# A fused attention and gated-MLP kernel: which VectorE steps GpSimd's pieces wait for, with the order of all engines made anew

## The chip, the core and the metric

The kernel runs on one core of a Trainium2 chip. Five engines of that core work side by side and meet by semaphores: TensorE (PE, with its weight loads shown as PEld), VectorE (DVE), ScalarE (ACT), GpSimd (POOL) and SyncE (SP), which here issues nearly all DMAs. The metric is the device time of one execution in microseconds.

## The reference, cut to what matters

Eight batches of eight heads, 576 positions, head size 64; inputs are float32. Attention has a decay that comes from the running sum of log f, and its output goes through a gated MLP whose gate is a causal convolution of five taps.

```python
def _attn_ref(q, k, v, f):
    ...
    scores = scale * np.matmul(q, k.transpose(0, 1, 3, 2))
    log_f = np.log(np.clip(f, 0.0001, 1.0))
    cum = np.cumsum(log_f, axis=-1)
    decay = cum[:, :, :, None] - cum[:, :, None, :]
    scores = np.where(causal, -1000000000.0, scores + decay)
    ...
    attn = attn / (np.sum(attn, axis=-1, keepdims=True) + 1e-09)
    return np.matmul(attn, v).astype(np.float32)

def _moe_ref(x, w_val, conv_w, w_out):
    ...
    for k in range(K):
        gate_pre += conv_w[k][None, None, :] * xp[:, k:k + S, :]
    gate = 1.0 / (1.0 + np.exp(-gate_pre))
    val = x @ w_val
    return (gate * val @ w_out).astype(np.float32)
```

## The kernel before, in words

The 64 heads are worked as 32 pairs; one pair fills the 128 partitions. The program is a list of some 2350 steps, each a small Python function that issues one or a few instructions. Each pair i goes through these steps, named by their class in the code:

- S: PE multiplies q and k into PSUM banks in 64-row blocks and adds the decay, which it takes as a product of the selector pk with st, three bf16 pieces of the scaled running sum. For the first pair these two are apart (S and Sd).
- red: VectorE's custom instruction (L423) applies the mask and takes the row maximum (negm). SX: ScalarE takes the exponential (L427) into P and sums it into zs.
- DT: VectorE turns P in 32x32 blocks into T (L462). UC: two copies of T's halves into U (L248, on ACT, POOL or DVE), and U: four DMAs of the other halves.
- rec: 1e-9 is added to the sums (L435, on POOL or DVE); VectorE takes the reciprocal (L439) and turns it into zt (L440). zD and zB: DMAs that spread the reciprocals over zb.
- PV: PE multiplies U and v. X: VectorE multiplies the result by zb into x (L519).
- xh and xl: x is split into a part that PE takes in one pass and the rest (L248, L528). conv, cvm, cva: the five taps of the gate, one product (L255 on POOL and DVE, L253 on ACT) and one addition (L564 on POOL) each, or both in one on VectorE (L562). tanh: ScalarE.

After every fourth pair a batch is complete: Mv multiplies xh and xl with w_val, H (L595) applies the gate, hh and hl split the result (L609), Mo multiplies with w_out, O empties the bank and OD stores it. At the start come the steps on f: the clip and the running sum (class st0, L325 and L337), their scaling on ACT, and three casts with two subtractions in between (cast, L248, and st0, L345); for the last eleven pairs the same is done once more in the middle of the program (sts[1]), from a copy in DRAM (lnf). The two weight matrices are decoded from their int32 halves in many steps of ACT, VectorE and POOL (wv and wo; L695 to L711), beside the first pairs.

The order in which the steps are issued is neither a loop nor decided by the chip. A packed table, ORDER, holds for each place in the program the number of a step and the engine that does it (for those steps that may go to more than one), and behind that the PSUM banks. Every engine works through its own instructions strictly in that order and halts at the first whose semaphores are not there.

One rule is added when the steps are issued. PORT is a set of class names. The last VectorE instruction of such a class so far is kept in turn, and the first instruction of every POOL step gets a semaphore wait for it:

```python
        if e == "POOL" and turn is not None:
            tc.add_manual_dep(done[0], turn.name, wait, reason="shared port")
        elif e == "DVE" and cls in PORT:
            turn = done[-1]
```

Before, the class rec covers the addition of 1e-9 and also VectorE's step of reciprocal and turn, so a POOL step that comes behind such a step in the table waits for its turn zt (L440). The classes st0 and cast are not in the set.

Of the kernel before, what the change touches and what calls it, by code (L numbers as in the profile page):

```python
# [90 lines left out]
)
# [702 lines left out]
```

## Time and profile before

| | us |
| --- | --- |
| median of three timed runs | 459.16 (458.07 to 460.58) |
| profiled execution | 463.08 |
| its span, first to last instruction | 461.0 |
| mean granted TensorE clock | 0.981 |

The durations below come from the one profiled execution, which took 3.9 us more than the median. A row in order of time gives start and duration in us, the engine, the line, what was written from what, and in brackets how long the engine had stood idle before and on whom it had waited. A busy PE is not PE at its peak, since matmuls are pipelined and their ends are modelled.

### The profile page before, as it was taken

Reading aid. Unit: us, or ns where it says so; the run is one execution under the profiler, and the core shown is the slowest. Engines: PE = TensorE matmul, PEld = TensorE weight load, DVE = VectorE, ACT = ScalarE, POOL = GpSimd, SP = SyncE. Lnnn points to the kernel's source line nnn. Section 1 sums busy time; section 2 is a strip of 40 time slices with the busy share of each in tenths; the row PEclk is TensorE's granted clock in tenths of the full one; section 3 lists DMA queues with packets and bytes.
Section 4 is the critical chain, followed back from the end, with each engine's and each line's share of the span. In section 5 each row is a group of like instructions: output and inputs, shape, how many; then the busy total and the mean of one; then the engine's idle time right before and its main releaser. Section 6 shows DMA issues by size and latency. Waiting matters only on the chain.

```text
span 461.0 us, 16758 instructions
## 1 busy us (share of the span) xinstructions
PE 423.9 (92%) x6640; PEld 359.9 (78%) x6640; DVE 382.9 (83%) x1034; ACT 332.3 (72%) x836; POOL 309.4 (67%) x310
## 2 busy tenths in 40 slices
PE   6648998899999999999969898999999999999996
PEld 6427777787888788898858677988787988999985
DVE  5998987998997798999869888899777879976851
ACT  5786996999886878987667868677678878654131
POOL 7476756678884868787536889589579888572210
PEclk9797999999999999999989999999999999999999
DMA  8748879848695767987773587768587686845013
GB/s 287 283 129 249 213 190 241 198 118 261 186 248 163 209 171 197 274 232 206 211 199 100 136 239 215 219 181 204 132 246 192 188 206 173 223 118 129 23 70 114
DMA packets 74847, 87.23 MB, mean 189 GB/s; under 512 B 48145, under 2 KB 48145, under 8 KB 74769
## 3 DMA queue, kind: packets, MB, share of 16 engines
q1 hardware_dynamic: 74624, 85.87, 67.7%
q8 instruction: 52, 0.85, 0.9%
q10 hardware_dynamic: 144, 0.29, 0.2%
q14 instruction: 27, 0.21, 0.2%
HBM read 52.29 MB, written 10.26 MB: 136 GB/s over the span
## 4 chain that ended last, share of the span: by engine, by line
PE 47%; POOL 13%; DVE 13%; DMA 12%; issue 6%; SPq 5%; ACT 3%; POOLq 0%; DVEq 0%; ACTq 0%
PE banks L233 47%; POOL gate L564 6%; SPq L260 5%; DMA zb<-zd 4%; DVE banks L423 4%; DVE T L462 3%; DMA U<-T 2%; DMA vt<-in_v_dram 2%; POOL xl L528 2%; POOL U L248 2%; ACT P L427 2%; DMA sh<-in_w_val_dram 1%; POOL tm L255 1%; DMA zd<-zt 1%; DMA tm<-lnf 1%
## 5 line engine op out<-in xcount | busy, mean ns | idle before, releaser
L427 ACT ACTIVATE P<-banks,negm 128x384 f32<-128x384 f32 (+8 forms) x288 | 149.6, 528 | 46.4 <-DVE negm L423 36.4
L564 POOL TENSOR_TENSOR gate<-gate,tm 128x576 f32<-128x576 f32 x82 | 117.5, 1434 | 42.6 <-DVE tm L255 14.7
L423 DVE CUSTOM_DVE_ANT_0 banks<-banks,mk 128x512 f32<-128x512 f32 (+8 forms) x288 | 135.1, 504 | 9.6 <-PE banks L233 6.7
L462 DVE STREAM_TRANSPOSE T<-P 128x1088 f32<-128x1088 f32 (+2 forms) x96 | 110.9, 1166 | 6.6 <-DMA U<-T 3.5
L233 PE MATMUL banks<-xh,wall 128*128 128x288 f32 x512 | 108.8, 298 | 1.7 <-ACT P L427 0.9
L233 PE MATMUL banks<-Xr 64*64 64x288 f32 (+8 forms) x1280 | 103.2, 410 | 2.5 <-DMA Xr<-in_x_dram 2.5
L233 PEld LDWEIGHTS banks<-U,vt 64*64 64x64 f32 x3456 | 92.3, 136 | 14.1 <-issue 10.1
L233 PE MATMUL banks<-U,vt 64*64 64x128 f32 (+1 forms) x3456 | 93.2, 257 | 9.6 <-ACT sh L695 4.0
L233 PE MATMUL banks<-wall,hh 128*128 128x512 f32 x288 | 91.6, 399 | 0.0
L233 PEld LDWEIGHTS banks<-xh,wall 128*128 128x128 f32 x512 | 84.3, 189 | 6.0 <-ACT P L427 1.6
L233 PE MATMUL banks<-xl,wall 128*128 128x288 f32 x256 | 76.0, 297 | 4.1 <-POOL xl L528 3.9
L233 PEld LDWEIGHTS banks<-Xr 64*64 64x64 f32 x1280 | 65.0, 134 | 15.8 <-issue 5.1
L233 PEld LDWEIGHTS banks<-wall,hh 128*128 128x128 f32 x288 | 52.3, 189 | 13.2 <-DVE negm L423 1.3
L233 PE MATMUL banks<-st,pk 64*64 64x288 bf16 (+8 forms) x640 | 48.6, 297 | 11.3 <-ACT P L427 6.5
L233 PE MATMUL banks<-wall,hl 128*128 128x512 f32 x144 | 56.9, 395 | 2.3 <-POOL hl L609 2.3
L427 ACT ACTIVATION_READ_ACCUMULATOR P<-banks,negm 128x1 f32 x288 | 58.4, 203 | 0.0
L248 ACT COPY U<-T 128x1440 f32<-128x1440 f32 x37 | 51.3, 1396 | 5.9 <-PE banks L233 5.2
L233 PEld LDWEIGHTS banks<-xl,wall 128*128 128x128 f32 x256 | 48.4, 189 | 5.4 <-POOL xl L528 4.1
L233 PEld LDWEIGHTS <-pk 64*64 64x64 bf16 x640 | 26.5, 107 | 29.6 <-issue 24.9
L609 POOL TENSOR_TENSOR hl<-h,hh 128x576 fp32r<-128x576 f32 (+2 forms) x39 | 40.9, 1068 | 11.5 <-DVE gate L562 4.4
L528 POOL TENSOR_TENSOR xl<-x,xh 128x576 fp32r<-128x576 f32 x24 | 34.7, 1446 | 15.9 <-DVE zt L440 10.4
L519 DVE TENSOR_TENSOR x<-banks,zb 128x256 f32<-128x256 f32 (+1 forms) x96 | 30.8, 345 | 11.5 <-PE banks L233 5.5
(103 smaller groups left out, 495.8 us busy)
## 6 DMA issues: line engine op xcount, KB each, us to landing
U<-T SPq DMA_DIRECT2D x128, 180.0 KB
Xr<-in_x_dram SPq DMA_DIRECT2D x64, 288.0 KB
vt<-in_v_dram SPq DMA_DIRECT2D x32, 320.0 KB
out_dram<-ot SPq DMA_DIRECT2D x36, 256.0 KB
vt<-in_v_dram SPq DMA_DIRECT2D x32, 256.0 KB
zb<-zd SPq DMA_DIRECT2D x64, 80.0 KB
zb<-zd SPq DMA_DIRECT2D x64, 64.0 KB
sh<-in_w_val_dram SPq DMA_DIRECT2D x2, 512.0 KB
```

Source lines behind the costliest of these rows:

```text
L233: nc.tensor.matmul(out, lhsT=lhsT, rhs=rhs, start=start, stop=stop)
L248: (eng.copy if eng is nc.scalar else eng.tensor_copy)(out=out, in_=in_)
L255: eng.tensor_scalar(out=out, in0=in_, scalar1=col, scalar2=0.0, op0=ALU.mult, op1=ALU.add)
L260: lambda e: (nc.sync if e == "SP" else nc.scalar).dma_start(out=out, in_=in_), reads, writes, dma=span)
L423: nc.vector.tensor_tensor_reduce(out=sl, in0=sl, in1=mk[:, S - ext:], op0=ALU.add, op1=ALU.min, scale=-0.125, scalar=3.0e38, accum_out=neg ...
L427: nc.scalar.activation(out=dst, in_=bank(key)[:, a0:a0 + ext], func=AF.Exp, bias=negm[r][:, col], scale=-1.0, accum_out=zs[r][:, col])
L462: nc.vector.transpose(out=bass.AP(Tt.tensor, Tt.offset + 32 * FB[js[0]], [pitch, (32, nk), (CW, 2), (1, 32)]), in_=Pt[u])
L519: nc.vector.tensor_tensor(out=bass.AP(to.tensor, to.offset, [to.ap[0], *dims, (1, D)]), in0=bank(keys[y])[:, D * first:D * last].rearrange ...
L528: any_("xl", {"POOL": 1.4, "DVE": 0.67}, p, lambda eng: eng.tensor_tensor(out=xl[s], in0=xv, in1=xh[s][:, :].bitcast(F32), op=ALU.subtract ...
L564: eng.tensor_tensor(out=gt, in0=gt, in1=to, op=ALU.add)
L609: eng.tensor_tensor(out=hl[jj][:, y:y + x1 - x0], in0=h2[jj % 2][:, x0:x1], in1=hh[jj][:, y:y + x1 - x0].bitcast(F32), op=ALU.subtract)
```

## The change

Three things: the set PORT gets st0, cast and a name vdup that no step has; VectorE's step of reciprocal and turn gets the class recT, which is not in the set; and ORDER is another table. A POOL step so no longer waits for reciprocals and their turn, and waits for VectorE's clip, running sum, casts and subtractions on f where they come ahead of it in the table. The addition of 1e-9 keeps its class rec.

```diff
-PORT = {"wv", "wo", "rec", "xh", "xl", "diag", "conv", "cvm", "cva", "hh", "hl", "UC"}
+PORT = {"st0", "cast", "vdup", "wv", "wo", "rec", "xh", "xl", "diag", "conv", "cvm", "cva", "hh", "hl", "UC"}
 NS = (21, 11)
 ORDER = (
...
-    "c-lQuTTB$`wyvtKzTd0w)%WWAy}SB;@2<Y14~RYp@-QGL5##~UohW*e0o{o(JP5-{1bG;clL&GWKp%v0Cj-Mt6gi0^I}vmeL3bkPB*J(SK~8d{?U{%A>tAbq>s#wv>xV"
...
+    "c-mD`c}QIOmae<hzVB7H_FMa2b!*?NZtW%y)Z~w7JJ8xbh{gxT_CYimXe)UTZ3onLAQ}f+<3M73pmqkL?LccBh{ge99Ec_j(PSW+JV@+3h{iuADeVVyFPGmv=X~co-#N"
...
         def turn():
             nc.vector.reciprocal(out=zr[r][:, 0:NN], in_=zr[r][:, 0:NN])
             nc.vector.transpose(out=zt[r], in_=zr[r])
-        dve("rec", 0.36, p, turn, [("zr", r)], [("zr", r), ("zt", r)])
+        dve("recT", 0.36, p, turn, [("zr", r)], [("zr", r), ("zt", r)])
```

What the new table does is read from the instructions of the two programs, engine by engine. First POOL at the start of the program. ident is the unit matrix, one a column of ones that L337 reads, mk the mask, pk and sel the selectors of the decay. Before:

```order
L283 AFFINE_SELECT ident<-ident 128x128
L293 MEMSET one 128x1
L363 MEMSET zr_93 128x32
L362 MEMSET x_99 128x4
L314 MEMSET mk 128x576
L317 AFFINE_SELECT mk<-mk 64x64 x2
L294 MEMSET ebias 128x1
L298 MEMSET pk 128x64
L299 MEMSET sel 128x4
L305 AFFINE_SELECT pk<-pk 128x21 x3
```

Now, from the last rows of pk on; sh and wall are the weight decoding, U the copy of T:

```order
L305 AFFINE_SELECT pk<-pk 128x11 x3
L309 AFFINE_SELECT sel<-sel 64x1 x2
L293 MEMSET one 128x1
L314 MEMSET mk 128x576
L317 AFFINE_SELECT mk<-mk 64x64 x2
L707 TENSOR_TENSOR wall<-sh 128x512
L701 TENSOR_TENSOR sh<-sh 128x512
L363 MEMSET zr_93 128x32
L363 MEMSET zr_94 128x32
L536 TENSOR_TENSOR tm<-ident,cw 128x640
```

The constant one has moved from ahead of the mask to behind the whole of pk and sel, and so have the mask and the first zr and x; the first weight piece is L707 instead of L701.

Second, POOL in the middle, around the second round of the steps on f; the numbers tell the buffers apart (xl3 is the low part of the last pair of batch 3, U1 and zr1 belong to the pair after the next). Before:

```order
L564 TENSOR_TENSOR gate_113<-gate_113,tm_78 128x576 x3
L528 TENSOR_TENSOR xl1_108<-x321_100,xh1_102 128x576
L435 TENSOR_SCALAR zr1_94<-zs1_92 128x9
L528 TENSOR_TENSOR xl2_109<-x320_99,xh2_103 128x576
L248 COPY U1_85<-T1_83 128x1440
L528 TENSOR_TENSOR xl3_110<-x321_100,xh3_104 128x576
L255 TENSOR_SCALAR gate_113<-x321_100,cw_65 128x576
L564 TENSOR_TENSOR gate_113<-gate_113,tm_78 128x576 x2
L609 TENSOR_TENSOR hl_1439<-h320_114,hh_1262 128x64
```

Now:

```order
L435 TENSOR_SCALAR zr0_93<-zs0_91 128x9
L528 TENSOR_TENSOR xl1_108<-x321_100,xh1_102 128x576
L255 TENSOR_SCALAR tm_78<-x320_99,cw_65 128x576
L564 TENSOR_TENSOR gate_113<-gate_113,tm_78 128x576 x2
L435 TENSOR_SCALAR zr1_94<-zs1_92 128x9
L248 COPY U1_85<-T1_83 128x1440 x2
L255 TENSOR_SCALAR gate_113<-x321_100,cw_65 128x576
L564 TENSOR_TENSOR gate_113<-gate_113,tm_78 128x576
L255 TENSOR_SCALAR tm_78<-x321_100,cw_65 128x576
```

The pieces xl2 and xl3 are no longer among POOL's, and both copies into U1 have come to stand there together.

Third, VectorE at the same place. Before (the second instruction of each L423 is left out, as it repeats):

```order
L519 TENSOR_TENSOR x321_100<-banks_122,zb1_98 128x2x2x64 x2
L337 SCALAR_TENSOR_TENSOR tm_78<-one_123,tm_78 128x576
L339 TENSOR_SCALAR ref1_125<-tm_78 128x1
L423 ISA banks_122,negm0_89<-banks_122,mk_73 128x128
L423 ISA banks_122,negm0_89<-banks_122,mk_73 128x256
L423 ISA banks_122,negm0_89<-banks_122,mk_73 128x448
L248 CAST st1_71<-tm_78 128x576
L423 ISA banks_122,negm0_89<-banks_122,mk_73 128x320
L345 SCALAR_TENSOR_TENSOR tm_78<-st1_71,sel_72,tm_78 128x576
L423 ISA banks_122,negm0_89<-banks_122,mk_73 128x64
L439 RECIPROCAL zr1_94<-zr1_94 128x9
L440 STREAM_TRANSPOSE zt1_96<-zr1_94 128x32
```

Now:

```order
L519 TENSOR_TENSOR x321_100<-banks_122,zb1_98 128x2x2x64
L519 TENSOR_TENSOR x321_100<-banks_122,zb1_98 128x64
L519 TENSOR_TENSOR x321_100<-banks_122,zb1_98 128x2x2x64
L423 ISA banks_122,negm0_89<-banks_122,mk_73 128x448
L439 RECIPROCAL zr1_94<-zr1_94 128x9
L440 STREAM_TRANSPOSE zt1_96<-zr1_94 128x32
L423 ISA banks_122,negm0_89<-banks_122,mk_73 128x64
L528 TENSOR_TENSOR xl3_110<-x321_100,xh3_104 128x576
L337 SCALAR_TENSOR_TENSOR tm_78<-one_123,tm_78 128x576
L339 TENSOR_SCALAR ref1_125<-tm_78 128x1
```

The reciprocal and its turn now come ahead of the running sum L337 instead of behind it, and so does xl3, which was POOL's.

## Rows read from the trace of the kernel before

**Rows 1.** The page's busy us, share of the span and instructions of each engine.
```profile
PE 423.9 (92%) x6640; PEld 359.9 (78%) x6640; DVE 382.9 (83%) x1034; ACT 332.3 (72%) x836; POOL 309.4 (67%) x310
```

**Rows 2.** Ten-us windows: stretch, length, busy us: PE, PEld, DVE, ACT, POOL.
```profile
10.00:20.00 10.00, 5.70 (x70) 4.00 (x65) 9.67 (x26) 7.38 (x16) 4.32 (x3) 0.71 1.01 374
230.00:240.00 10.00, 6.11 (x30) 5.29 (x29) 5.82 (x17) 7.18 (x17) 2.68 (x2) 0.83 0.87 229
```

**Rows 3.** Order of time, first 16 us (start, duration, engine, line, what).
```profile
2.69 0.15 POOL L298 MEMSET pk<- 128x64 bf16 x1
...
5.87 1.35 DVE L337 TENSOR_TENSOR_SCAN x<-one,gate 128x576 f32<-128x576 f32 x1
...
8.29 0.32 POOL L309 TENSOR_SCALAR_AFFINE_SELECT sel<-sel 64x1 f32<-64x1 f32 x2
...
9.66 0.46 DVE L248 CAST st<-gate 128x576 bf16<-128x576 f32 x1 [0.23 <-ACT gate L341]
...
10.25 1.95 DVE L345 SCALAR_TENSOR_TENSOR gate<-st,sel,gate 128x576 f32<-128x576 bf16 x1
...
10.29 1.29 POOL L701 TENSOR_TENSOR sh<-sh 128x512 f32<-128x512 f32 x1 [1.69 <-ACT sh L699]
...
12.23 1.43 DVE L248 CAST st<-gate 128x576 bf16<-128x576 f32 x1
...
13.77 0.82 DVE L345 SCALAR_TENSOR_TENSOR gate<-st,sel,gate 128x576 f32<-128x576 bf16 x1
...
15.13 1.43 PE L233 MATMUL banks<-st,pk 64*64 64x288 bf16 x20 [3.13 <-DVE st L248]
```

**Rows 4.** Order of time up to PE's first matmuls on U.
```profile
22.62 2.10 DVE L462 STREAM_TRANSPOSE T<-P 128x768 f32<-128x768 f32 x2
...
26.82 1.38 POOL L248 COPY U<-T 128x1440 f32<-128x1440 f32 x1 [2.54 <-DVE zt L440]
...
30.86 1.18 SPq L260 DMA_DIRECT2D U<-T  x2
...
36.79 4.98 PE L233 MATMUL banks<-U,vt 64*64 64x128 f32 x105 [4.03 <-ACT sh L695]
```

**Rows 5.** Order of time at PE's halt in the middle.
```profile
227.13 0.67 ACT L248 CAST xh<-x 128x576 fp32r<-128x576 f32 x1
...
232.90 0.21 DVE L440 STREAM_TRANSPOSE zt<-zr 128x32 f32<-128x32 f32 x1
...
233.26 1.45 POOL L528 TENSOR_TENSOR xl<-x,xh 128x576 fp32r<-128x576 f32 x1 [5.60 <-DVE zt L440]
...
234.77 0.40 PE L233 MATMUL banks<-xl,wall 128*128 128x288 f32 x1 [3.89 <-POOL xl L528]
```

**Rows 6.** Two-us windows after the halt; behind POOL the granted clock.
```profile
236.00:238.00 2.00, 2.00 (x7) 1.51 (x6) 0.46 (x1) 1.06 (x4) 0.00 (x0) 0.52 0.96 288
238.00:240.00 2.00, 2.00 (x11) 1.90 (x10) 0.14 (x1) 1.41 (x5) 0.00 (x0) 0.63 0.82 209
```

**Rows 7.** Waits of POOL: who waited for whom, us in total, times, longest.
```profile
POOL xl L528 <- DVE zt L440: 10.4, 5, 5.6
```

**Rows 8.** Waits of PE, same columns.
```profile
PE banks L233 <- POOL hl L609: 2.3, 1, 2.3
```

**Rows 9.** Lines L439 and L440: smallest, median, largest ns.
```profile
L439 DVE RECIPROCAL zr<-zr x32: 170/207/217, 26.3 to 411.6; 128x9 f32<-128x9 f32 x32
L440 DVE STREAM_TRANSPOSE zt<-zr x32: 210/211/215, 26.5 to 411.9; 128x32 f32<-128x32 f32 x32
```

**Rows 10.** Order of time where a reciprocal falls inside a POOL addition.
```profile
109.71 1.43 POOL L564 TENSOR_TENSOR gate<-gate,tm 128x576 f32<-128x576 f32 x1
...
110.16 0.17 DVE L439 RECIPROCAL zr<-zr 128x9 f32<-128x9 f32 x1
```

**Rows 11.** Costliest groups: the gate additions on POOL and on DVE.
```profile
L564 POOL TENSOR_TENSOR gate<-gate,tm 128x576 f32<-128x576 f32 x82 | 117.5, 1434 | 42.6 <-DVE tm L255 14.7
L562 DVE SCALAR_TENSOR_TENSOR gate<-x,cw,gate 128x576 f32<-128x576 f32 x38 | 32.2, 855 | 6.1 <-POOL gate L564 5.8
```

More of the change, by code (lines that the diff above doesn't have):

```diff
@@ new lines @@
+    "5G|Bz2iQORghkh-Zm)U?X&kbecFx+9dCiC#V=00(oEswTCJNzb5XJtEd>Inb=88gZCM~P`kissurvO&wy!4h|*7OBR(hHBh^ytsrBG6b(Fe9in8{oThtZm4&yzwliEe~"
+    "vgS$6U=R3~)DPYSZxBa`kEz?#3zRP6_e2lv5NxK-Q4gsE@^!`s5(M2Qz9J1Uj!0f=9i@eQmcoEeQ!awL3@UA(aloLFd1QpV&hU_j7?(ka7N${{n~Z6q8)~DBF;M0rgU7"
+    "^}jg&hKF0{;;VT^$Y6ox8UwJb9;#0-+9Opu8)HRKdo1J$!q&|UB{^GC`WtBQGzam2nt$<S;xm?NNFqYP4-S$nK4R*CtZb&=Ie8KKB&I$D(a9jljlnl?w7V;!<)D8sBCm"
+    "X&OUPBFJx3oL+LAWyJHS^caDN`Z3<s)oLTrdi!k6}btbvD-K+tP<xet&vto`<1dlNwc3&{ze&q9#L*^&eLW%73?uiJF|_}%^89^I3-#qtqt0t%yPPEcQ_r;B4?SCq!Z{"
@@ new lines @@
+    "8&H=?le@**=R-mtP2buFw9rFs~EPIJN&TL_JvKpC_OfDPcm^rtgt55?6<AgZXoN9U#r-nnJzoWV66VN{81(!$1IS}=bw#WSm8lq9D9G-<&!IQGX^g}M6x&ZA#E6{uHf6"
+    "zv00PiuBVcCR@>=yP2a~paOO)(dl>zuE7Qfintz^S3@*r!>|yeQktZfDoA@6x<N8(T{Mjy}g+VRrITye?i3?-^9Z>*t-Pe}d*{ApBpn=iDRF3XKNScnI$o`bAzV{UQA}"
+    "{V`2T@1$R+5738s+Z+wg&3i_hqHoiN=$o8x=$F_%>;blbQ(|8d&P#653qm^g32&V~N8hBsq`zUlWHtz!gb#%S!fIhHuOy@}UekHpec=$hM)*PW8*`NRfwLo=5pozCTm}"
+    "c`jtSR=TfAHBPfUn)AnX<n2_G|`F^@R!=x;f4?veyy9MJCwXN4Sbn=m7M#q)Bb+<QDke21qIFA6Q<P2sLEDORwOTqcXha*L<gpr~1VQ4BM#A$?*KqrkY!Mp<0Zuy|BV7"
@@ new lines @@
+    "1fHXxpU%9@q~C<Tp_L(cZqFW9e18r!L1Uz7-7Z(b}jd3c0`1WVE!s^iC4+ciQe*bj3eF$-f0m-92G8z!{VosN9=9(Iq4JjGxi(yzGO$TE1~dv#4BR2sGfTuk&A31SllS"
+    "uko+^3$8V4#e2TOeS(V^YlwXp5%e}xYacdZ6RwLtIxJ9X%-z~+YA?bTI#{W02T5z5Jg8w7`A%B2-n?J?{r99~xzmFf{KNfHCQE8J@D*Y?hEKT!Y^UsPX0!VU-|4iH_-R"
+    "BSUXZQ#FS$;j=B;W{UxE<12?iv0A{v+vE{0n@Vq*}U$&}4@QSGI-hA+N-MY(w!uTqhb)eapYhZx#KBw1|$x8HPaeR=lbhkYWNvu#JpL-y@JfEh~w7MC($UWCAG&z7~W8"
+    ")5sjMfK&>?GK;K2c3v>3T0uHRUHmH9Yeib%l{}X&Np%vrq)~Guy(b++`b8;Ot)NZNA=p=(R|X{q3bzbYwkZ+WkW`|ql?^CMN>o`b!IjqqL(1ENzluhXd1<|jsx&Kq7Tp"
@@ new lines @@
+    "y6AiFB)6WkKbh$<wQ5|?x+ABbK_ABmobrUW5nlWa&ZESplz3Vsz$O1qUjWwT^QR3qt<%&FQW3o4hoT3Mr9QN5LZkXES2lmw(*_E=R^HYo2XU#M!;hpN{C8gg0kz2pbUH"
+    "Q6)eO-WddsA=k6*>lB`ph~S#bJcq)9)ch{%3aYz!8^g4U|e=ZHZGWy-IG0(0qSogKPk6VOR`sr4MUw~Ubd=i*KR1^D*s(FA*oltS7{J8av<0eq|`;kqTZ6N%PwhlWF^h"
+    "6Y(TT599KOz94W2Hv}8yVLDI-a&23G$<~LbEeqCNE|5}cseexgWiy9F9C*+p;lWa%RtTv-FnsrUBoQF=RTeKI|QgmJks|M8!)u!gWyhFXKnN*Fa@2PLgDZ(?zpO6Nm4F"
+    "TnJ`LbqKLq%ugV;YToSl%Yb(CgX(?U1%ZeqYO%UqEGYtGo^6sK&H+wAa)hl)dV!@*VBEc3*?4-10?j2&L#YwY%D7ZM$Z~WKkh1RQF1-uU%4OI-V{f??BRMT6IPHLjF*$"
@@ new lines @@
+    "R$M`0VT)#7y(Xt9IKn@u4zwX%N^aJ<RW+(Dxk<rMRI8d)Qr(;!)XivL%OA+UQ6UOUu`h2mzB3%iJ5;!?)7WJkHjWyl!ieg!?pxJW)l>B#dKw)!okcg)b?7y;#nOnDbcc"
+    "o><Er|M4lsrky}A*UW>gz@)O+fFV^LRO+*j8ctBm!=19dO@BN{YYj1$JNaR!}0Q^waOu5k{<%?;)zv)j0Uj_az;kODF8o33daEp@tf-K1_rrxUj5_!_!KtEn-|G--uZ^"
+    "U`?V^cX#_Xf`gImQASHY%ZGDO?$>^Bc$<ZvYJ;0p82+-RZ&p5^p%PZ#inTmtx-%V!kS;v9kfDoi2e=TN9kJ7EH!^;Y1FklKNzbtJ0?g=H6NH}jePB0^IOA|&TE5B*A#;"
+    "~ofb3qScWaLihj$KWlp!EThy%@H;m7XSDZ&ig7vz7&N5?Ov9#(R>$Y@K?WkqJ(x)%zmy80F&1TVJ+BWkgy~Vm`*|N~AA?;&JN?W0=*4AoE`gTjD{<<Ql?^AHCZfm#dp{"
@@ new lines @@
+    "-GIpxd^*x76x!{jh#WF|L?2O<3x+ySjp{+9om8*y{C&wZXP;(^%JSqx!4n%jPB<W<pJ2>!$6%c4$diFWGi%ySA6Q-*kiKd2_FMz*e%2*=B5XeYb7McE>hro6<kjQw(eR"
+    "cl!JKar1~7(qGVT>G}FLE9_yI+H9THMZH3QSN~DZF`#;jsn0p=yk~l0HtV<bhygT!_ED$CuxR_nv|(N{XKWnTs(H`+i!<teZa!s=*x%?g?z7gY&1%>;PdE>qE6y$Fo-^"
+    "#KG+eXRSsSe_)+*B}(^sYorfbe61=k)jQSH-Cm*LQixN!S9!<^INdhFbG1`VJ^XaBRQ(}Wv%miNw-%k8Q+oO3^Q11^p0FQy*TY5RzE)oZhR?Q(mA`?`D4J?5@(wYggjQ"
+    "j6I#Zf&t^EglQqa@E!34q5sPmkepsjGN}#cY|1m`@r3Ax?!MVv+hRw70YdFi{Z4P*UIqpxOUtF?jd){eae!yoU!b>m)&>VgH|3^XCHK(wa-`=t#j6OcdNZ*uX2?PqlRV"
@@ new lines @@
+    "cSFS6rc2}e8rS%l{#M)`!v`VoS*SJgV`O#D9sj*l*Zcne_@75msfPK!h;A!^Uw7VP>$2<Fq=dowPQ|syR1RWpk1qa7b@44vFV7KgVtYJ^5C*|q#Y<Q!=DZ^Q}4V!dDu|"
+    "q4@R_W;XOnZ8rprgWrIB>_7ry8qu414YyUVHbw5+7uv+hn#o_F4Og>nHmIJKtOHShhd0KeJzO+;<&#U)pgW;>CQ`KG0X=^I~v#(vZRGuzRjW*Lfe+SM-H^8i&<U^2t4?"
+    "-K!CAaKN|jLVex7cB}=vg6X{5o}-Y!(}=COc)mSXn{UXs<?8ThY`b=|@9(Zd*P`K>@1?8NG39vZxbC>`xa3%K^f}goW4@AO%kf<h_IkaqyczEYkIf6YcRj<7Q3u_9*Kr"
+    "sGLOZ^#U{7!_xaer`eTP*B2e9VgcJO_0+o5&8aSUVAK8E*Vus`_LcjTE1)&}c?!@-H*XmC3C&H?+Ee5-~HU(|co$8mmi0M3PAXRrs8g!yind(~G6Tixl<PuMIrirvK+&"
@@ new lines @@
+    "UxRF@41&2!op}c6gGzo-Wy@JyA*B+SBF=E(ojwK5%vIU3U6Xhu$S0kxFS^RbvfI@)n0yRCOj5y@Xm%M&Y%-@;$hs`5$+BzhZ+74zNN^E$X?{@Xiu~`IuO1S-o@6#zhU&"
+    "qWiQ8%`rk*Iya!l+v@`mz-iy($=(paNVNSF+b~ZE^d!Eb$y&+wwF%%8)A{!A~=xHn*Mf?>}i{I^!_zxpM)aH~&P6t~;bs<Z1KZZnk@ts(E2#(kyjPPH)JziZT8gWN8(W"
+    "+=FI_$mWz3V;YpY{$%YooXQul;NOK7Y#p&VT3!<EFq3f2H%Of6Bib+YBGX&N=7&JN_~M&)(ZHTGSMuiQ(}x{#ySyUhkB~sqqDGF+LmHNRHrd!_On$$Wi!1cs;rmZOOcf"
+    "o_1ae{mH)=J0GYFEXTg_FZf5J9eykh26{rYKq=Jbzv{1!4}{iZXuKxg8sG$60ZHIo;F14MR1glu8{$Ku)>Jsq?e7dU1iAufAQ`zCZ;Fq_t0Tjy&eXf)PocY^pF`gV9)w"
@@ new lines @@
+    "0yOVNALipXlTCzT5Hr_`ybKyBnO`9Gn)KsaSdRRn-kD%F*`7_UgZO-{z=qb<(+fst5a=53Uga;Lbd8-d!?cx*JV5cm*%6nYuj3L&Xr8c#Q*CsJ_iT6{7vAHR=Zj=Txo3"
+    "jIr@K2o2mN?nY+OkIt<#;eo3bW{3WU@h=5u!yhY#dJ-28NU!g)6J>9)INSY@iefBQ)1rSy|_6oO>YN!<Ad>|=xTg5uoS-%ABccyYWe^Nf^P#KQupxb)KbcpV+42bw)D*"
+    "iFNVgDSSWTkax3yvBo#XoI~DsbBfvLOgzQ?pC)1z7(zNVw#*&?ljApjtJMp{e+0<TqDzlYAvMZUc^i2A4`m5M>Mw4}C--o!_=c)PhY6`|*CI1-fP4^`@!MV&r#uD3)AI"
+    "8roB*Dr=TMUccNSsSdC0Y|;qB*vg(F7l7-e<neUXF#cV~M#$L*hziB2&m!=N{%7a<T+9v5;Wk{Dd~~C}B-_66?9n#C~okcbKWkN$}3B1@B69#hP-d>~3x;eUzHSN794o"
@@ L91 @@
+    "f9HF|eFNF0+9rXt13Bg%LbKlRtk@xfZFMLnyO<d5Gl`F7tjtfn^U|_I*Kq(FvSHe%Aq%RT9ftq%tR1j>BaHP)3r<Sn`Pya+wV(=aI`<<Z=#F#{S;VF$YlY|5zVbp4IP|"
+    "WBeCo$0|r=6ja6^{~u2RD0gsd!6&MZeP7s!WyOS(E`bw;@Cgz;sZK0U^Z0I#l@rT|<9^9yKlG1@{XSEud}qXyO22mpp7i}CLMYpWva;hzAM1fmw1Z^~RK}9Z(;%GOA$("
+    "$kC;gMk5%S4Yj(LFc^o|uA=O0h(c)$Mto*efNp0NIY!|(|sq3k=ZalAjkKep<a1vuH+V<cFv`hTkx)${"
 )
```

53 lines of the change are left out of this document (7 added, 46 removed).

## The prediction

> **What bounds the kernel now.** I read the page's busy times first, then the windows of ten us, then who ended PE's and POOL's waits, and last the order of time at the places where PE stood still. The busy times [rows 1] show PE at 423.9 of 461.0 us; DVE has 382.9, POOL 309.4. So the matmuls set the time, and an edit is worth what it takes from PE's 37.1 idle us or from its slow clock. The windows [rows 2] show where the idle time is: 4.3 of the ten us from 10 to 20, with DVE busy for 9.67 of them, and 3.9 of the ten from 230 to 240; most other windows are nearly full.
>
> At the start the chain is DVE's: the running sum of the decay (L337, 5.87), its three bf16 pieces (L248, L345), and then the first matmul that needs them, at 15.13 [rows 3]. In the middle PE stops at about 230.9 and goes on at 234.77, when POOL's piece xl (L528) is there; POOL had stood 5.60 us for the turned reciprocals (L440, 232.90 + 0.21), although the operand xh was done at 227.13 + 0.67 = 227.80 [rows 5]. POOL's xl pieces wait for L440 five times, 10.4 us in all [rows 7]. These are the waits for VectorE's reciprocals that the change names.
>
> **The change, part by part.**
>
> *The wait for the reciprocals goes.* It is the wait in [rows 5]. In the new order the xl piece at this place is done by VectorE itself, right after the pair's X pieces and the turn and ahead of the running sum. With xh at 227.8 and a piece of about 0.8 (the row of the same shape with three operands, L562, has a mean of 0.855 [rows 11]) xl is there at about 228.7, before PE runs dry at 230.9. That gives PE 3.9 us. The halt also cost clock: in 236:238 and 238:240 PE ran, right after standing, at 0.52 and 0.63 of the full clock (mostly the lower level of 1.2 GHz), busy throughout [rows 6], so (1 - 0.52) x 2 + (1 - 0.63) x 2 = 1.7 us of work was lost there. Both go together: -5.6. The bounds are 0 (another piece of the same product is late) and -5.6. I take -5.6, because the row names one releaser and it is removed.
>
> Whether the wait protected something is asked of the reciprocals themselves. L439 lasts 170/207/217 ns and L440 210/211/215 ns, smallest, middle and largest of 32 each [rows 9]; a reciprocal that fell inside a POOL addition of 1.43 us at 109.71 took 0.17 [rows 10]. So running them beside POOL costs nothing that the trace can show: 0, and as the other bound what the casts suffer, which makes a rival below.
>
> *The new wait for the first steps on f.* The second of the three casts took 1.43 where the first took 0.46, the first L345 1.95 where the second took 0.82, both while POOL ran weight pieces from 10.29 on [rows 3]. Kept apart, the chain loses 0.97 + 1.13 = 2.1 us. Against that stands the move of the constant `one`, which L337 reads: it now comes behind POOL's whole table pk. That table ran to 8.61 (8.29 + 0.32) from 2.69 [rows 3]; the mask, zr and x pieces that stood ahead of it now stand behind it, so it ends by 8.6 at the latest, and L337 is put off by at most 8.61 - 5.87 = 2.7 us. Between L337's end and the first cast lay 2.4 us (5.87 + 1.35 = 7.22 to 9.66), of which ScalarE's step takes less than one; the rest was waiting, so the table's earlier start decides between a cost of 0 and some 1.3. I take 0.3. Gain at 15.13: 2.1 - 0.3 = 1.8, so 13.3. What is queued behind the waiting POOL pieces is the weight decoding and then the two U copies of the first pair, for which PE's first U,vt matmuls wait (36.79 [rows 4]). POOL's first weight piece now starts after the casts and two weight pieces of VectorE, at about 14.2 (13.3 and two pieces of a cast's 0.46) instead of 10.29. Up to the end of the second U copy POOL then has six weight pieces or their like of 1.29 (L701 [rows 3]) and two copies of 1.38 [rows 4], with small ones some 11 us, so 25.3 if nothing waits. The copies cannot start before the last transposes, at 24.7 (22.62 + 2.10 [rows 4]), minus what the shorter chain gives. Before, the first of them started at 26.82, after 2.54 us of waiting for L440, and the U transfers of the second were issued at 30.86. Now two copies after 24.7 end at about 27.5, some 3 us before 30.86. PE's first U,vt matmuls so gain between 1.8 and 3.1; the bounds for the end are 0 and -3.1, and I take -1.8, since DVE is the full engine here [rows 2] and what it gains is the chain's 1.8.
>
> *A rule of the Trainium skill, weighed.* The rows: L345 began at 10.25, 0.04 us before POOL's L701, took 1.95, and L701 took 1.29 like its kind [rows 3]. The Trainium skill (SBUF — State Buffer, Who interferes with whom) says that the pair of ports which VectorE and GpSimd share is an exclusive lock, and that whichever of the two starts first keeps it for the whole instruction. By that POOL should have been the one to stand, and the chain would gain only the cast's 0.97; the trace has VectorE lengthened by 1.13, close to L701's length, so I keep 2.1. The same rule of the Trainium skill speaks against the change: one of the two waits in any case, and a semaphore only chooses which.
>
> *The order made anew.* Counted in the two programs' instructions, POOL goes from 315 to 301 and VectorE from 1036 to 1047; five of POOL's 82 gate additions (1.434 each) become VectorE's (0.855 each [rows 11]). VectorE's added work is between 5 x 0.855 = 4.3 and 11 x 0.855 = 9.4 us. It lies beside PE as long as VectorE's 78 idle us cover it, so I cost it at 0 and keep 9.4 as the price without cover. POOL loses at least 5 x 1.434 = 7.2 us, which is slack unless POOL is late: PE's wait for hl, 2.3 us [rows 8], is such a place. A table of 2354 steps drawn anew also has waits that the old one had not. I count one of 2.3, the largest that PE had in the main stretch beside the one of [rows 5], and leave the old hl wait where it is.
>
> *Sum:* -5.6 - 1.8 + 2.3 = -5.1. The profiled execution took 463.08 us (span 461.0), so it would take 458.0. The median of the three timed runs is 459.16, 3.9 below the profiled one; the same difference leads from 459.16 to 454.1.
>
> **The rivals.**
>
> *The halt in the middle stays.* xl is now VectorE's, and VectorE takes its pieces in turn: if a piece ahead of it (a row of softmax, or the reciprocal, which needs POOL's sums) is late, PE stands at the same product for as long. For: the new order leaves PE only a few pieces there. Against: 2.2 us lie between 228.7 and 230.9. Then 454.1 + 5.6 = 459.7.
>
> *VectorE becomes the bound (slower).* Place: the gate additions and low-half pieces taken over from POOL. Price: up to 9.4. For: VectorE is at 9.67 of 10 early on [rows 2]. Against: 83% over the span [rows 1]. It decides from where more than 461.5 - 454.1 = 7.4 us of them find no cover; in full, 454.1 + 9.4 = 463.5.
>
> *The reciprocals collide after all (slower).* If they were held as the cast was, 32 pairs at POOL's 67% share [rows 1] with half a POOL addition each (0.7) give 15 us of VectorE; half of it uncovered leads to 461.6. The rows of the reciprocals speak plainly against [rows 9, 10].
>
> *The new wait only moves the loss to POOL.* POOL's late start eats the 1.8 at the first U copies: 454.1 + 1.8 = 455.9. For: its first pieces start 3.9 us later. Against: it waited 2.54 us at these copies before [rows 4], and that wait is gone. By the lock rule of the Trainium skill (same page and section) this would be the outcome.
>
> *Better still.* No new wait of 2.3, and the hl wait goes too with a POOL that is less loaded: 454.1 - 4.6 = 449.5.
>
> **How the numbers follow.** Forecast 0.45, with 451 to 457 as its own range; the loss moved to POOL 0.08; better still 0.09; the halt stays 0.18; VectorE as the bound 0.17; collisions 0.03. 0.5% of 459.16 is 2.3 us, about what a measurement of this kernel tells from no change: faster means under 456.9, slower over 461.5. The first three cases lie below 456.9 but for a small tail that I give to "same": faster 0.59, same 0.21, slower 0.20. The range for 8 in 10 runs from 449 to 461.5, which leaves out most of the last two cases and a little of the best one.
>
> **What would show it.** Right: PE's row near 230 without an idle stretch of 3 us, and the windows there at full clock; both L345 near 0.82 and all casts near 0.46 at the start; the first matmul on st near 13.3 and the first U,vt matmuls by 35; L439 and L440 as short as before, with no POOL row that waits for them. Wrong: a PE wait on xl or hl of more than 3 us, the first U,vt matmuls later than 36.8, a DVE share over 85% with PE's idle time ended by DVE, or lengthened reciprocals.

## The result and the profile after

| | before | after |
|---|---|---|
| median, us (lowest to highest of 4 runs each, on one chip) | 458.7 (458.07 to 460.58) | 440.1 (438.8 to 441.98) |
| ratio, 95% interval | | 0.9591 (0.9545 to 0.9637) |
| profiled execution / its span, us | 463.08 / 461.0 | 440.2 / 438.5 |

The change gives 18.6 us. The forecast was 454.1 with a range of 449 to 461.5: the direction is right, the size is not, and the time lies outside the range. Medians here and below are of all runs of a kernel, while ratios leave out those that were over 1.5% above its fastest, so a ratio and a median need not match (0.9555 and 442.18 below).

The page's busy times of the kernel after, as in [rows 1]:

```profile
PE 417.3 (95%) x6640; PEld 356.5 (81%) x6640; DVE 376.0 (86%) x1045; ACT 335.5 (77%) x834; POOL 286.3 (65%) x296
```

PE has the same 6640 matmuls. Its idle time is 438.5 - 417.3 = 21.2 us instead of 37.1, so 15.9 of the 22.5 by which the profiled spans differ are idle time; the other 6.6 are busy time. (The spans differ by 3.9 more than the medians, as the profiled execution of before took 4.4 more than its median.) The windows say where. First the two of [rows 2], now of after:

```profile
10.00:20.00 10.00, 6.65 (x72) 4.91 (x75) 9.83 (x30) 9.81 (x25) 5.28 (x7) 0.66 0.82 289
230.00:240.00 10.00, 10.00 (x178) 9.52 (x178) 8.91 (x25) 7.71 (x24) 7.40 (x10) 1.00 0.81 212
```

PE's halt in the middle is gone, and with it the low clock behind it (1.00 instead of 0.83). Longer stretches of the kernel before (stretch, its length, busy us of PE, PEld, DVE, ACT, POOL, the granted clock, DMA share, GB/s):

```profile
0.00:50.00 50.00, 33.22 (x413) 25.56 (x414) 41.67 (x123) 36.13 (x95) 30.22 (x57) 0.86 0.74 233
50.00:150.00 100.00, 94.12 (x1650) 79.69 (x1652) 89.87 (x250) 86.02 (x217) 72.34 (x62) 1.00 0.77 202
...
225.00:245.00 20.00, 16.11 (x215) 14.11 (x211) 13.93 (x34) 11.12 (x27) 9.07 (x8) 0.91 0.65 173
245.00:300.00 55.00, 51.12 (x840) 43.46 (x832) 47.84 (x136) 41.26 (x110) 41.62 (x41) 1.00 0.70 192
```

and of the kernel after:

```profile
0.00:50.00 50.00, 36.20 (x538) 27.01 (x539) 43.56 (x128) 40.73 (x105) 33.55 (x61) 0.93 0.80 250
50.00:150.00 100.00, 99.22 (x1662) 84.09 (x1664) 92.89 (x270) 88.61 (x222) 74.53 (x72) 1.00 0.81 216
...
225.00:245.00 20.00, 20.00 (x377) 17.79 (x370) 17.77 (x55) 16.14 (x39) 16.87 (x20) 1.00 0.86 223
245.00:300.00 55.00, 53.35 (x851) 44.93 (x853) 47.03 (x132) 43.32 (x113) 41.63 (x37) 1.00 0.77 193
```

The place that the prediction priced (225 to 245) gives 3.9 us of idle time. The stretch from 50 to 150, of which it said nothing, gives 5.1, the first 50 give 3.0, and 245 to 300 gives 2.2. The stretches do not hold quite the same work, but the sign is plain: the gain is spread. Of the busy time, the clock returned at most some 50 x 0.07 = 3.5 at the start and 20 x 0.09 = 1.8 in the middle, an estimate from the clock's column alone; at the start PE stood still for 14 to 17 of the 50 us, and a low clock costs nothing there.

What ended PE's waits in the kernel after (who waits, for whom: us, times, longest), the five largest of eight rows; POOL's xl [rows 5] and hl [rows 8] are in none of the eight:

```profile
PE banks L233 <- ACT P L427: 7.1, 12, 2.1
PE banks L233 <- issue: 2.8, 2, 1.5
PE banks L233 <- DVE st L248: 2.7, 1, 2.7
PE banks L352 <- POOL ebias L294: 1.4, 1, 1.4
PE banks L233 <- DMA Xr<-in_x_dram: 1.2, 1, 1.2
```

The order of time at the start, as in [rows 3, 4], and at the place of [rows 5]:

```profile
6.86 1.38 DVE L337 TENSOR_TENSOR_SCAN x<-one,gate 128x576 f32<-128x576 f32 x1
...
9.26 0.46 DVE L248 CAST st<-gate 128x576 bf16<-128x576 f32 x1 [0.47 <-ACT gate L341]
9.76 0.82 DVE L345 SCALAR_TENSOR_TENSOR gate<-st,sel,gate 128x576 f32<-128x576 bf16 x1
...
10.61 0.46 DVE L248 CAST st<-gate 128x576 bf16<-128x576 f32 x1
...
12.47 0.81 PE L233 MATMUL banks<-st,pk 64*64 64x288 bf16 x20 [2.67 <-DVE st L248]
...
13.34 0.69 DVE L423 CUSTOM_DVE_ANT_0 banks<-banks,mk 128x512 f32<-128x512 f32 x1
...
13.72 1.29 POOL L707 TENSOR_TENSOR wall<-sh 128x512 fp32r<-128x512 f32 x1 [5.45 <-ACT sh L705]
...
33.35 0.38 PE L233 MATMUL banks<-U,vt 64*64 64x128 f32 x2
...
215.69 0.75 DVE L528 TENSOR_TENSOR xl<-x,xh 128x576 fp32r<-128x576 f32 x1
...
217.56 0.29 PE L233 MATMUL banks<-xl,wall 128*128 128x288 f32 x1
```

The steps on f run at their undisturbed lengths, the first matmul on st comes 2.66 us earlier, the first on U 3.4 (33.35 for 36.79). xl of the place in the middle is done at 216.44, 1.1 us before PE first takes it (217.56, the first of PE's products that reads this buffer in the order of the program).

### The profile page after: what moved, and what is told of

Its sections match the earlier page's. It is cut to its first block, busy times and chain, and to the rows that moved or that the text cites. A ratio compares the mean times of both kernels' runs of the same rounds, so it can differ in the third digit from the quotient of the medians.

```text
span 438.5 us, 16745 instructions
## 1 busy us (share of the span) xinstructions
PE 417.3 (95%) x6640; PEld 356.5 (81%) x6640; DVE 376.0 (86%) x1045; ACT 335.5 (77%) x834; POOL 286.3 (65%) x296
## 4 chain that ended last, share of the span: by engine, by line
PE 84%; DVE 6%; DMA 5%; issue 3%; SPq 1%; ACT 1%; POOL 0%; DVEq 0%; ACTq 0%; POOLq 0%
PE banks L233 84%; DVE banks L423 2%; DMA U<-T 2%; DVE T L462 2%; DMA sl<-in_w_out_dram 1%; DMA sh<-in_w_val_dram 1%; SPq L260 1%; DVE gate L345 0%; DVE negm L423 0%; DVE h L595 0%; DVE st L248 0%; DVE x L337 0%; POOL wall L711 0%; ACT ot L636 0%; DMA vt<-in_v_dram 0%
## 5 line engine op out<-in xcount | busy, mean ns | idle before, releaser
L427 ACT ACTIVATE P<-banks,negm 128x512 f32<-128x512 f32 (+8 forms) x288 | 149.6, 528 | 39.9 <-DVE negm L423 29.5
L423 DVE CUSTOM_DVE_ANT_0 banks<-banks,mk 128x512 f32<-128x512 f32 (+8 forms) x288 | 134.8, 506 | 16.3 <-PE banks L233 12.5
L564 POOL TENSOR_TENSOR gate<-gate,tm 128x576 f32<-128x576 f32 x77 | 109.5, 1424 | 46.8 <-DVE tm L255 11.0
L462 DVE STREAM_TRANSPOSE T<-P 128x1024 f32<-128x1024 f32 (+2 forms) x96 | 110.9, 1166 | 7.9 <-DMA U<-T 3.0
L233 PEld LDWEIGHTS banks<-U,vt 64*64 64x64 f32 x3456 | 89.6, 133 | 6.8 <-ACT P L427 1.6
L233 PE MATMUL banks<-U,vt 64*64 64x128 f32 (+1 forms) x3456 | 91.0, 253 | 2.5 <-ACT P L427 1.0
L248 ACT COPY U<-T 128x1440 f32<-128x1440 f32 x44 | 61.2, 1396 | 6.2 <-PE banks L233 3.2
L233 PE MATMUL banks<-st,pk 64*64 64x256 bf16 (+8 forms) x640 | 47.8, 293 | 9.6 <-ACT P L427 6.1
L255 POOL TENSOR_SCALAR tm<-x,cw 128x576 f32<-128x576 f32 x36 | 27.7, 770 | 19.9 <-DVE gate L562 16.9
L423 DVE DVE_READ_ACCUMULATOR2_ANT negm<- 128x1 f32 x288 | 40.1, 139 | 0.0
L609 POOL TENSOR_TENSOR hl<-h,hh 128x576 fp32r<-128x576 f32 (+2 forms) x34 | 35.6, 1063 | 6.5 <-ACT tm L253 2.6
```

Of the source, the lines that this page charges most:

```text
L233: nc.tensor.matmul(out, lhsT=lhsT, rhs=rhs, start=start, stop=stop)
L248: (eng.copy if eng is nc.scalar else eng.tensor_copy)(out=out, in_=in_)
L255: eng.tensor_scalar(out=out, in0=in_, scalar1=col, scalar2=0.0, op0=ALU.mult, op1=ALU.add)
L423: nc.vector.tensor_tensor_reduce(out=sl, in0=sl, in1=mk[:, S - ext:], op0=ALU.add, op1=ALU.min, scale=-0.125, scalar=3.0e38, accum_out=neg ...
L427: nc.scalar.activation(out=dst, in_=bank(key)[:, a0:a0 + ext], func=AF.Exp, bias=negm[r][:, col], scale=-1.0, accum_out=zs[r][:, col])
L462: nc.vector.transpose(out=bass.AP(Tt.tensor, Tt.offset + 32 * FB[js[0]], [pitch, (32, nk), (CW, 2), (1, 32)]), in_=Pt[u])
```

## The experiments

All times in us; "ratio" is to runs of the kernel before on the same chip, with its 95% interval. The medians of before beside these runs were 458.1 to 459.7, so medians of this section can be compared within about one us. The change has three parts: the reciprocals' wait out, the wait for the steps on f in, the table. The first eight runs put them together in other ways.

| table | reciprocals' wait | wait on f | median | ratio |
|---|---|---|---|---|
| old | in | out (before) | 458.7 | 1 |
| old | out | out | 442.79 | 0.9682 (0.9633 to 0.9731) |
| old | in | in | 461.25 | 1.0085 (1.0043 to 1.0126) |
| old | out | in | 449.52 | 0.982 (0.9772 to 0.9868) |
| old | PORT empty | | 443.22 | 0.9655 (0.9605 to 0.9706) |
| new | in | out | 446.73 | 0.975 (0.9707 to 0.9792) |
| new | in | in | 445.94 | 0.9691 (0.9642 to 0.974) |
| new | out | out | 442.18 | 0.9555 (0.9479 to 0.9632) |
| new | out | in (after) | 440.1 | 0.9591 (0.9545 to 0.9637) |
| new | PORT empty | | 442.0 | 0.9626 (0.9586 to 0.9665) |

**Old table, both edits of the rule.** The kernel before with

```diff
-PORT = {"wv", "wo", "rec",
+PORT = {"st0", "cast", "vdup", "wv", "wo", "rec",
...
-        dve("rec", 0.36, p, turn, [("zr", r)], [("zr", r), ("zt", r)])
+        dve("recT", 0.36, p, turn, [("zr", r)], [("zr", r), ("zt", r)])
```

> The table of before with both edits of the rule (reciprocal and turn out of the set, st0 and cast in it). Theory A, the waits for the reciprocals were the cost: most of the 18.6 us comes with the rule alone, 440 to 449. Theory B, the table is the gain: 455 to 460, the halt at 230 shorter at best. Theory C, rule and table gain only together: 451 to 456, that is the halt in the middle and the start, as my prediction had it.

449.52, just above the range of theory A. The rule alone gives half of the gain, and the next two runs show that this is a large gain and a loss together.

**Old table, only the second of the two edits** (recT).

> The table of before, only the reciprocal and its turn leave the set. Theory A: within 2 us of the kernel with both edits. Theory B: 456 to 460. Theory C: 452 to 457, the first casts still lengthened by POOL (1.43 and 1.95), the halt of 3.9 us near 230 gone or under 2.

442.79: 15.3 us (458.11 - 442.79) from one word in one line, nearly three times the 5.6 that the prediction gave this term, with the old order of every instruction. It lies below the ranges of all three theories.

**Old table, only the first of the two edits** (st0 and cast in PORT).

> The table of before, only st0 and cast join the set; the reciprocals are still waited for. Theory A and C: 456 to 459, the two casts at the start at their 0.46 and 0.82, the first matmul on st near 13.0, the halt near 230 still there. Theory B: the same as before, 457 to 460.

461.25, above both ranges and slower than before by 0.4 to 1.3%. So in the old table the wait on f costs 3.1 on top of the old rule, and 449.52 - 442.79 = 6.7 on top of the other edit.

**New table, the old rule.** The kernel after with both edits undone.

> The new table under the old rule: POOL waits again for reciprocal and turn, and not for the first steps on f. Theory A: 452 to 460, most of the gain lost. Theory B: 440 to 444. Theory C: 445 to 452.

446.73: the table alone gives 11.4 (against 458.1 of the same chip). With the 15.3 this would be 26.7, and the whole change gives 18.6, so the two are in good part the same gain. Under the old rule POOL waited 39.1 us on L439 and L440 in the old table and 25.4 in the new one (sums of the rows of its waits). The rows of the kernel before, beside the 10.4 of [rows 7]:

```profile
POOL tm L255 <- DVE zt L440: 6.7, 3, 3.4
POOL gate L255 <- DVE zt L440: 6.5, 2, 3.8
POOL gate L564 <- DVE zt L440: 5.6, 3, 3.8
POOL tm L255 <- DVE zr L439: 3.9, 1, 3.9
POOL U L248 <- DVE zt L440: 3.7, 2, 2.5
POOL gate L564 <- DVE zr L439: 2.3, 1, 2.3
```

The two on L439 are not the rule's: they stand, at 6.0 together, in the old table with the turns out of the set too, and the others do not. So the turns held POOL for some 33 us.

**New table, no wait on f.** The kernel after with st0 and cast taken out of PORT.

> The new table, reciprocal and turn out of the set as now, but st0 and cast out too. If the wait for the first steps on f is a cost in any table (it took 3.1 and 6.7 us in the old one): 434 to 438. If the new table is laid out for it: 440 to 444, with casts at the start lengthened again to over 1 us. If it no longer matters: 439 to 441.

442.18, with runs from 436.57 to 443.43; the intervals of this ratio and of the kernel after lie over each other. The casts at the start are not lengthened, although no POOL piece waits for them:

```profile
9.76 0.82 DVE L345 SCALAR_TENSOR_TENSOR gate<-st,sel,gate 128x576 f32<-128x576 bf16 x1
...
12.47 0.81 PE L233 MATMUL banks<-st,pk 64*64 64x288 bf16 x20 [2.69 <-DVE st L248]
...
13.74 1.29 POOL L707 TENSOR_TENSOR wall<-sh 128x512 fp32r<-128x512 f32 x1 [5.47 <-ACT sh L705]
```

These are the starts of the kernel after to 0.02 us. In the new table POOL's first weight piece waits for ScalarE's data until 13.74, so the table by itself keeps the first steps on f apart from it; the run under the old rule and the one with PORT empty below have both L345 there at 0.82 too. What the wait on f does in this table is in the middle: without it one L345 of the second round takes 1.92 us, with it 0.82.

**New table, both waits.** The kernel after with recT made rec again.

> The new table, POOL waits for the first steps on f and again for reciprocal and turn. If the reciprocals' wait costs the new table what the kernel with the old rule showed: 446 to 449. If the wait for f hides part of it: 442 to 446.

445.94. Taking the reciprocals' wait out is worth 5.8 here (to 440.1); without the wait on f it is 4.5 by the medians (446.73 to 442.18) and 8.9 by the ratios (0.975 to 0.9555 of 458). The wait on f makes no difference that these runs can tell, in either pair.

**PORT empty, in the new and in the old table:** POOL never waits to keep off VectorE.

```diff
-PORT = {...}
+PORT = set()
```

> The new table with the set empty, so POOL waits for no VectorE step beyond its data. If the remaining waits keep VectorE's pieces from being lengthened and that is worth time: 444 to 456, with L562 and L528 on VectorE lengthened. If every such wait only costs: 432 to 438.

> The old table with the set empty. If the remaining waits are worth time: slower than 442.8, 444 to 455. If only data waits count: 436 to 441, as fast as the new table or faster.

442.0 and 443.22, both between the ranges of the two expectations. Without the rule VectorE's instructions are lengthened again, L562 up to 1.32 us in the new table and 2.04 in the old one, where with the turns alone out of the set the longest takes 0.82; L562 in the kernel after and in the old table without the rule (smallest, middle, largest ns of all, start of the first and last):

```profile
L562 DVE SCALAR_TENSOR_TENSOR gate<-x,cw,gate x43: 778/812/821, 69.5 to 415.4; 128x576 f32<-128x576 f32 x43
```

```profile
L562 DVE SCALAR_TENSOR_TENSOR gate<-x,cw,gate x38: 778/815/2036, 70.4 to 415.9; 128x576 f32<-128x576 f32 x38
```

Yet it costs no time that stands out: 442.0 stands against 440.1 and 443.22 against 442.79, in both pairs with intervals that lie over each other. So what the rule orders beside the turns gains nothing that these runs can tell, and one class in it cost 15 us.

**Where the 15.3 come from.** Three runs with the old table free only some pairs' turns. The first frees only the turn that ended POOL's wait in [rows 5]; the others have `i < 4` and `i >= 4 and i != 17` in its place:

```diff
-        dve("rec", 0.36, p, turn, [("zr", r)], [("zr", r), ("zt", r)])
+        dve("recT" if i == 17 else "rec", 0.36, p, turn, [("zr", r)], [("zr", r), ("zt", r)])
```

> The table of before; only the turn of pair 17 (the one before the halt near 230) no longer holds POOL. Theory A (the prediction's step: the halt is 5.6 of the loss, and it is all that the waits cost): about 453. Theory B (the waits cost PE time at many places, some 4 at the start, 5 at this halt, the rest elsewhere): also about 453. Rival C (POOL is late at the next place for the same reason, so that freeing one turn gives back little): 456 to 459. PE's wait on xl of 3.9 gone under A and B.

> The table of before; only the turns of pairs 0 to 3 no longer hold POOL. Theory A: 458.7, nothing. Theory B: PV of pair 0 starts 3.7 earlier, as it did where all turns were freed (36.5 to 32.8), of which 2.1 were left by pair 3, so 455 to 456.6. Rival C: the lead is lost by pair 9, 458 to 459.

> The table of before; the turns of pairs 4 to 16 and 18 to 31 no longer hold POOL. Theory A: 458.7, since the halt near 230 and the start stay. Theory B: the rest of the 15.3 that freeing all gave, less some 2 to 4 at the start and 5 at the halt: 6 to 8, so 451 to 453, with no single PE wait of over 2 us gone for it. Rival C: less than 3, 456 or more.

| turns freed | median | less than 458.77 by | ratio |
|---|---|---|---|
| pair 17 | 453.44 | 5.3 | 0.9869 (0.9842 to 0.9896) |
| pairs 0 to 3 | 457.52 | 1.3 | 0.9983 (0.9952 to 1.0014) |
| the other 27 | 449.99 | 8.8 | 0.9778 (0.9746 to 0.981) |
| sum | | 15.4 | |
| all (second run above; less than its own 458.11) | 442.79 | 15.3 | |

The parts add up: 15.4 by the medians, and by the ratios 17.0 against 14.6, within their intervals. Pair 17 fits theories A and B and rules out C, pairs 0 to 3 lie between the ranges of B and C, and the other 27 are beyond the range of B, with a PE wait of over 2 us gone that B had not expected (hl, below). So the term for the halt was right by itself; the pairs at the start give little (the ratio's interval holds 1); and more than half of the gain lies where the prediction had put nothing. The traces show at which places. In the table each row is a stretch of the program, from the first matmul on U of one pair to that of another (read from the order of time), with its length in the five traces: three in which the turns of that stretch still held POOL, two in which they did not.

| stretch | held (mean) | freed (mean) | gain |
|---|---|---|---|
| start to pair 0 | 36.8, 36.4, 36.0 (36.4) | 32.7, 33.1 (32.9) | 3.5 |
| pair 0 to 3 | 31.0, 30.5, 31.0 (30.8) | 33.5, 32.6 (33.0) | -2.2 |
| pair 3 to 4 | 17.5, 16.6, 16.7 (16.9) | 14.8, 15.7 (15.2) | 1.7 |
| pair 4 to 15 | 136.3, 135.1, 134.4 (135.3) | 133.1, 133.4 (133.2) | 2.0 |
| pair 15 to 16 (turn 17) | 18.9, 19.3, 19.1 (19.1) | 13.4, 13.7 (13.5) | 5.6 |
| pair 16 to 18 | 28.5, 29.2, 30.0 (29.2) | 25.8, 26.5 (26.1) | 3.1 |
| pair 18 to 24 | 74.2, 71.6, 71.1 (72.3) | 75.0, 71.1 (73.0) | -0.7 |
| pair 24 to 31 | 79.7, 79.5, 80.9 (80.0) | 78.0, 77.8 (77.9) | 2.1 |

At pair 16 to 18 the gain is a wait on POOL's hl; this row of the trace in which only pairs 0 to 3 were free stands, with the same 2.3, in the traces of before [rows 8] and of pair 17 alone, and in neither of the other two:

```profile
260.50 0.50 PE L233 MATMUL banks<-wall,hl 128*128 128x512 f32 x1 [2.30 <-POOL hl L609]
```

Two more come and go with it: a wait of 1.0 on VectorE's h between pairs 4 and 15, and one of 1.25 on ScalarE's P ahead of pair 25. From that trace, with what POOL, VectorE and ScalarE had waited for ahead of them:

```profile
137.77 2.92 POOL L564 TENSOR_TENSOR gate<-gate,tm 128x576 f32<-128x576 f32 x2 [3.83 <-DVE zt L440]
140.73 0.82 DVE L562 SCALAR_TENSOR_TENSOR gate<-x,cw,gate 128x576 f32<-128x576 f32 x1 [2.83 <-POOL gate L564]
...
144.64 0.27 PE L233 MATMUL banks<-st,pk 64*64 64x192 bf16 x4 [1.02 <-DVE h L595]
...
330.38 0.75 POOL L255 TENSOR_SCALAR gate<-x,cw 128x576 f32<-128x576 f32 x1 [2.73 <-DVE zt L440]
...
350.50 0.68 ACT L569 ACTIVATE gate<-gate 128x576 f32<-128x576 f32 x1 [2.15 <-POOL gate L564]
351.08 0.46 ACT L427 ACTIVATE P<-banks,negm 128x256 f32<-128x256 f32 x1
...
351.68 3.00 PE L233 MATMUL banks<-U,vt 64*64 64x128 f32 x108 [1.26 <-ACT P L427]
```

Here PE's row names VectorE or ScalarE, and yet the wait goes when POOL is freed. The rows show the links. POOL stood 3.83 us for the turn zt, VectorE 2.83 for POOL's gate, and VectorE's h, which starts at 144.17, came late to PE. At the second place POOL stood 2.73 for a turn and then worked without an idle stretch of 0.1 us until ScalarE had its gate; ScalarE had stood 2.15 for that, and its P came late to PE. The single links were not freed one by one. At the start 3.5 us are won at the first pair and 2.2 of them lost by the fourth, which is the 1.3 of the run.

**Why the wait on f costs in the old table.** In the trace with the old table and both edits POOL stands for the second round of steps on f, and PE for POOL (POOL's rows, then PE's):

```profile
224.51 0.24 POOL L435 TENSOR_SCALAR zr<-zs 128x9 f32<-128x9 f32 x1 [5.09 <-DVE ref L339]
224.83 1.40 POOL L528 TENSOR_TENSOR xl<-x,xh 128x576 fp32r<-128x576 f32 x1
```

```profile
226.29 0.40 PE L233 MATMUL banks<-xl,wall 128*128 128x288 f32 x1 [1.29 <-POOL xl L528]
...
230.00 0.61 PE L233 MATMUL banks<-xl,wall 128*128 128x288 f32 x1 [3.05 <-POOL xl L528]
```

The last run keeps both edits and the old table, but lets only the first round of those steps hold POOL (also at L339, L343 and L345):

```diff
-        dve("st0", 1.36, p, lambda: nc.vector.tensor_tensor_scan(
+        dve("stM" if n else "st0", 1.36, p, lambda: nc.vector.tensor_tensor_scan(
```

> The table of before, reciprocals' wait out, the wait for the steps on f in, but only for those at the start; the ones for the last eleven pairs, in the middle of the program, hold no POOL piece. Theory: the 6.7 by which the old table with the whole new rule (449.5) lay above the old table without any recip wait (442.8) come from one place in the middle, where POOL waited 5.09 for the middle block's running sum and PE for xl; so this is near 442.8, 441 to 445, with no PE wait on xl there. Rival: the wait costs at the start too, where PE waited 3.4 for P; then 446 to 450.

443.59 (ratio 0.9664, 0.9617 to 0.9711), and no wait of PE on POOL's xl: the 6.7 lay in the middle. The same trace shows why the wait at the start wins nothing in the old table although it does its work there:

```profile
9.83 0.82 DVE L345 SCALAR_TENSOR_TENSOR gate<-st,sel,gate 128x576 f32<-128x576 bf16 x1
...
12.81 1.50 DVE L703 TENSOR_SCALAR sl<-sl 128x512 int32<-128x512 int32 x1
15.48 0.43 DVE L709 TENSOR_SCALAR sh<-wall 128x512 int32<-128x512 int32 x1 [1.18 <-POOL wall L707]
15.82 0.76 DVE L423 CUSTOM_DVE_ANT_0 banks<-banks,mk 128x576 f32<-128x576 f32 x1
```

st is there at 12.6 instead of 14.8, but POOL's weight pieces start later, VectorE is held at L703 and waits for L707, and its first softmax row L423 stands behind both, at 15.82; without the wait on f it was at 15.67. In the new table that row stands ahead of those pieces and runs at 13.34, so there the start gains, with the wait on f or without it (13.35).

## Why the prediction was right or wrong

- *The wait for the reciprocals goes, -5.6.* This is the step that failed. At the place of [rows 5] it is right to 0.3 us (5.3 by the run that frees pair 17). But the term is the whole edit's, and that is 15.3. The bounds given were 0 and -5.6; they were bounds of one halt. 8.8 us came from the turns of 27 pairs to which the prediction gave nothing. The rows of POOL's waits showed more than one halt: 39.1 us on L439 and L440, some 33 of them the rule's, of which [rows 7] gave only the 10.4 of xl, the one piece that PE's row names at that halt. The other POOL pieces made VectorE and ScalarE late, and PE's row then carries their name.
- *Leave the old hl wait where it is.* Wrong: hl [rows 8] was late by the same wait, and freeing the turns removes it.
- *One new wait of 2.3 from the new table.* Wrong in sign. Under the old rule the table alone gives 11.4, and POOL stands less for the turns in it (25.4 for 39.1); how much of the 11.4 comes from that was not taken apart; once these do not hold POOL, what it adds, 442.79 to 440.1, is at the edge of what the intervals can tell. No PE wait after is as long as 2.3 but st's at the start.
- *Reciprocals beside POOL cost nothing.* Right. In the kernel after:

```profile
L439 DVE RECIPROCAL zr<-zr x32: 170/208/216, 24.0 to 396.5; 128x9 f32<-128x9 f32 x32
L440 DVE STREAM_TRANSPOSE zt<-zr x32: 211/212/215, 24.3 to 396.8; 128x32 f32<-128x32 f32 x32
```

  the lengths of [rows 9]. The rival of colliding reciprocals falls.
- *The steps on f apart, -1.8, first matmul on st at 13.3.* That the steps gain by being kept apart is right, and the local size a little small; that the new wait does it is wrong. In the new table without that wait the start is the same (12.47, L345 at 0.82), so the table does it, and the number came out near by luck. It is 12.47, both L345 at 0.82, POOL's first weight piece at 13.72 where 14.2 was said, the first U by 35 (33.35). From the first cast to the first matmul on st it took 15.13 - 9.66 = 5.47 [rows 3], now 12.47 - 9.26 = 3.21: 2.26 less, near the 2.1. The Trainium skill (SBUF — State Buffer, Who interferes with whom) has it that the first to start keeps the shared ports, which would have made it 0.97; for this pair, whose starts lie 0.04 us apart, the trace does not agree, while at the other eleven places of the trace of before where a VectorE instruction is more than a tenth longer than alone (L562, L528, L345, casts) POOL's piece had begun first. That it is worth 1.8 at the end is not shown: in the new table the wait on f makes no difference that the runs can tell. The rival that the loss moves to POOL is what happens in the old table, though in the middle (the 6.7) and not at the first U copies.
- *xl by VectorE, ahead of the running sum.* Right: it is there 1.1 us before PE needs it (2.2 was said), and the rival that the halt stays falls.
- *VectorE becomes the bound.* Falls. It carries five more L562 and 86%, over the 85% that was named as a sign, but PE's idle time is not VectorE's. Its busy time even fell by 6.9, since its instructions are hardly lengthened any more ([rows 11] gave L562 a mean of 0.855; now the largest is 0.821); 5.0 of that came in the old table with the turns alone freed (377.9). The pages count 310 and 296 instructions on POOL and 1034 and 1045 on VectorE where the prediction has 315 and 301, 1036 and 1047; the differences are the same.
- *The range.* Its lower end came from "better still", which added only the hl wait and the 2.3 to the forecast. A row for the edit as a whole, from all that POOL waited, had to stand beside it.

## What to carry to other kernels

A wait that is taken off an engine is priced by all that it holds there, not by the one halt at the engine that sets the time: add up the engine's waits on the releaser first, and take their full sum as the far bound, because late pieces reach the bound engine under other names. Here some 33 us of POOL's waiting for the turns were worth 15.3, since POOL then waited for other things: all its waits together fell from 122.5 to 104.6. A rule that orders two engines for the sake of a shared resource is worth trying empty: if its price lies on the path, it may cost more than the contention that it avoids.

## What the runs showed that was not expected

- Contention that can be seen and costs nothing that can be measured: with PORT empty VectorE's busy time rose from 376.0 to 381.9 (new table), and the time stayed within 2 us.
- Which instructions are lengthened beside POOL, in the old table with PORT empty: L562 (0.81 alone, up to 2.04), xl L528 (0.75, up to 1.75), the casts of st, xh and hh (0.46, up to 1.42), L345 (0.82, 1.66) and once the running sum (1.35, 2.44). The rows L423, the turns L462 in blocks, X (L519) and H (L595) kept theirs: one form of L519 takes 0.42 alone and beside POOL.
- The profiled lengths of one stretch differ between kernels in which nothing there was changed by up to 3 us (pair 18 to 24, held: 71.1 to 74.2), more than several of the gains; only the mean over several traces beside the timed runs tells these apart.
